# Talking-heads attention with a feed-forward block: other places for the loads of q, k, v and of the second weights, and for one batch's transposes

## The chip, the cores and the metric

The kernel runs on one core of a Trainium2 chip. Its time is the device time of one execution in microseconds. The kernel before took 603.37 us in the median of 13 runs, from 599.58 to 607.42.

## What is computed

For 8 batches of 12 heads with 448 positions of 64 elements, scores of all heads are mixed by a 12x12 matrix, go through a softmax, are mixed again by a second 12x12 matrix and multiply v. The result, 3584 rows of 768, goes through a feed-forward block with a squared ReLU and 2048 hidden columns.

```python
scores = scale * np.matmul(q, k.transpose(0, 1, 3, 2))
scores = np.einsum('bhij,hg->bgij', scores, w_pre)
scores = scores - np.max(scores, axis=-1, keepdims=True)
attn = np.exp(scores)
attn = attn / (np.sum(attn, axis=-1, keepdims=True) + 1e-09)
attn = np.einsum('bhij,hg->bgij', attn, w_post)
attn_out = np.matmul(attn, v)
...
h = np.maximum(x @ w_in, 0.0)
out = h * h @ w_out
```

All inputs and the output are float32 in memory; the loads convert to bf16 on the way into on-chip memory.

## The kernel before

**Tiles and pairs.** A tile is 10 query rows of one batch with all 12 heads, so 45 tiles make a batch and 360 make the whole. The main loop (L500) handles two tiles per pass, a *pair* `ds`; there are 180 pairs, 22.5 per batch, and a few closing passes. Loads are listed by tile number `i`, and tile `i` belongs to pair `i // 2`.

**One tile's way.** `load_qk` brings a third of the heads of k or q of a batch into the one staging tile `qkst` (L72 is where the DMA is issued, from GpSimd's queue, POOL). `turn_unit` transposes a third of the heads on TensorE (L182) and copies the result to `qT` and `kT` (L186, one copy on ScalarE and one on VectorE). `score_pair` (L319) computes scores of two heads for 128 rows (L329) and copies them to the tile `S` (L333). `gather` (L346, L357) is a DMA issued from SyncE's queue (SP) that reorders scores so that the 12 heads of a query lie on neighbouring partitions, in a tile `G`; there are 8 such tiles, and for the first 28 tiles of the run 6 more, which lie in the memory of the last quarter of the second weights (`w2_3`; the profile calls those gathers w<-S). `mix` (L361) multiplies a gathered pair by the first mixing matrix (L367), exponentiates on ScalarE (L372), takes the reciprocal of the sum on VectorE (L374) and scales on GpSimd (`d`, L376). `unmix` (L387), two pairs later (`LAG`), multiplies by the second matrix (L399) and copies to `at` (L404). When a third of a batch is unmixed, `av_unit` multiplies by v (L199), which gives columns of `xt`.

**The feed-forward block as filler.** Once a batch's attention is finished, its first feed-forward phase (`ffn1_unit`: products L251, ReLU on ScalarE L258, square on GpSimd L260) and then its second one (`ffn2_unit`: products L281, copy on VectorE L288, output DMA on SP's queue L271) are cut into units, and each pair runs some of them after its own work. So during most of the run each batch's pairs carry the feed-forward block of the batch before: from about pair 22.5 b + 5 to + 16 of batch b the first phase, from there to pair + 27 (the fifth pair of the next batch) the second one. In batch 0 the first phase of the batch itself runs in three parts as its columns become ready, up to pair 30; its second phase is from pair 30 to 49.

**What sets the order.** TensorE and GpSimd take their instructions in the order in which the program lists them (`manual_schedule`), so everything a pair lists on these engines, a load's issue included, stands in front of what follows. SP's queue holds gathers and output stores in order. `scores_for` issues at most one or two score pairs a pass, none in a pass that has a turn, and none whose heads have not been turned; `gathers_for` issues gathers up to 8 tiles ahead (14 in the head) and stops where scores are missing.

**Where the loads stand.** `at_load(i, ...)` puts a load at the start of the pass of tile i. Before the change:

| load | tile numbers | pairs |
|---|---|---|
| q, k of batch 1 (six thirds) | 9, 11, ... 19 | 4 to 9 |
| second weights (eight pieces of 256 rows) | 21, 23, ... 35 | 10 to 17 |
| v of batch 1 (four quarters) | 36 to 39 | 18, 18, 19, 19 |
| q, k of batch 2 | 40, 42, ... 50 | 20 to 25 |
| q, k of batch b + 2, b from 1 | 45 b + 22, ... + 32 | 22.5 b + 11 to + 16 |
| v of batch b + 1, b from 1 | 45 b + 34, ... + 40 | 22.5 b + 17 to + 20 |

`TURN` gives, counted from the pair in which a batch's tile 0 stands, the three pairs that turn the next batch's q and k: for the pair of batch 1 (pair 22) it is 7, 8, 9, so batch 2 is turned at pairs 29, 30 and 31.

Of the kernel before, what the change touches and what calls it, by code (L numbers as in the profile page):

```python
# [15 lines left out]
B, H, S, D = 8, 12, 448, 64  # L16
# [8 lines left out]
NT = 45  # L25
# [10 lines left out]
OFF = 64 - H * (IQ // 2)  # L36
SCALE = 1.0 / 8.0
FIRST_TURN = (15, 16, 17)
TURN = {0: FIRST_TURN, 1: (7, 8, 9), B: (1, 5, 8)}
EARLY = [10, 18, 25]  # L40
ROWS = [128, 128, 128, 64]

# [2 lines left out]
def kernel(  # L45
# [387 lines left out]
    with tc.manual_schedule(engines={PE, POOL}):  # L433
# [9 lines left out]
        def at_load(i, f, *args):  # L443
            loads.setdefault(i, []).append(lambda: f(*args))
# [2 lines left out]
            at_load(-1, load_w1, x)  # L447
        for x in range(4):
            at_load(-1 if x < 2 else 2, load_v, 0, x)
            at_load(36 + x, load_v, 1, x)  # L450
        for x in range(2, 8):
            at_load(1 + x, load_w1, x)
        for x in range(6):
            at_load(9 + 2 * x, load_qk, 1, x)
            at_load(40 + 2 * x, load_qk, 2, x)
        for x in range(8):
            at_load(21 + 2 * x, load_w2, x)
        for b in range(1, B):
            if b + 2 < B:
                for x in range(6):  # L460
                    at_load(NT * b + 22 + 2 * x, load_qk, b + 2, x)
            if b + 1 < B:
                for x in range(4):
                    at_load(NT * b + 34 + 2 * x, load_v, b + 1, x)
        nd = len(steps) // 2
        issued, gathered = [NPAIR + 3], [0]
        spans = [span_of(s) for s in steps]
# [32 lines left out]
        for ds in range(nd + LAG):  # L500
# [5 lines left out]
            for b, t in now2:  # L506
                if t == 0:
                    if b == 0:
                        at_step(ds + 6, (100, cg_unit))
                    if b + 1 < B:  # L510
                        for x in range(3):
                            turns[ds + TURN.get(b, TURN[B])[x]] = (b + 1, x)
            rest = ((NT + 1) // 2 + LAG + 2 - ds) % (NT / 2) + 1
# [70 lines left out]
```

## Time and profile before

| | |
|---|---|
| median of 13 runs | 603.37 us |
| profiled execution | 603.41 us |
| its span, first to last instruction | 601.6 us |
| mean granted TensorE clock | 0.978 |
| PE, DVE, ACT, POOL busy | 549.5, 409.2, 409.0, 400.2 us |
| software queue (loads, from POOL) | 23.60 MB, 29.4% of 16 engines |
| hardware queue of SP (gathers, output) | 49.35 MB, 35.6% of 16 engines |

PE is TensorE, DVE is VectorE, ACT is ScalarE, POOL is GpSimd, SP is SyncE; PEld is TensorE's loading of weights, which lies beside its matmuls. Engines work side by side, so the busy times don't add up to the span. A row of waits reads: engine, tile and line that waited, then what it waited for, total us, number of waits, longest. A row of groups reads: line, engine, operation, tiles, shapes, count, then busy us and mean ns of one, then the idle time before them and what ended it. These are rows for the instructions around the loads:

```profile
L376 POOL TENSOR_SCALAR d<-e_sb,rc 128x448 bf16<-128x448 f32 x360 | 226.5, 642 | 160.1 <-DVE rc L374 158.1
L260 POOL TENSOR_TENSOR h<-hr 128x448 bf16<-128x448 f32 (+2 forms) x136 | 114.0, 847 | 17.1 <-ACT hr L258 17.1
L72 POOL DMA_DIRECT2D qkst<-in_k_dram x24 | 16.0, 667 | 0.8 <-POOLq L568 0.8
L242 POOL DMA_DIRECT2D w<-in_moe_w_out_dram x8 | 6.0, 751 | 0.0
```

The last two are the time that GpSimd itself spends on issuing a load, not the time of the transfer.

### The profile page before, as it was taken

What the parts mean: (1) busy time and instruction counts of PE and PEld (TensorE: products, weight loads), DVE (VectorE), ACT (ScalarE), POOL (GpSimd) and SP (SyncE); (2) the same over time, 40 slices, a digit from 0 to 9 for tenths busy, and PEclk for the clock granted to TensorE, in tenths of its full rate; (3) what the DMA queues carried; (4) which work ended last, traced back from release to release, by engine and by line L of the source; (5) the groups of instructions that cost most, each with busy time, mean ns of one, the idle gap of its engine ahead of it and who ended that gap; (6) DMA issues with size and microseconds to landing.
All of it is one profiled execution on the core that took longest, in us unless ns stands there. A gap on an engine that the chain in (4) does not pass through costs nothing.

```text
span 601.6 us, 28171 instructions
## 1 busy us (share of the span) xinstructions
PE 549.5 (91%) x11810; PEld 312.2 (52%) x11810; DVE 409.2 (68%) x1050; ACT 409.0 (68%) x1223; POOL 400.2 (67%) x599
## 2 busy tenths in 40 slices
PE   3767788887999999999999999999999999999996
PEld 1534556643555455545555455545655555555554
DVE  6675577877886777766877687677877788754101
ACT  3656577876788767887688667876788768862420
POOL 5475577657568964898469954897478856882540
PEclk9888698999999999999999999999999999999999
DMA  9899999549755885489646885489543765442102
GB/s 141 134 222 186 190 171 170 98 64 188 161 123 112 152 159 122 98 136 144 142 109 106 148 165 112 88 151 159 128 102 73 122 145 122 80 76 66 30 17 76
DMA packets 83364, 74.98 MB, mean 125 GB/s; under 512 B 6436, under 2 KB 80164, under 8 KB 83236
## 3 DMA queue, kind: packets, MB, share of 16 engines
q1 hardware_dynamic: 51582, 49.35, 35.6%
q0 software_dynamic: 31264, 23.60, 29.4%
q8 instruction: 92, 1.51, 1.0%
q10 hardware_dynamic: 390, 0.22, 0.1%
q14 instruction: 36, 0.29, 0.1%
HBM read 47.20 MB, written 11.01 MB: 97 GB/s over the span
## 4 chain that ended last, share of the span: by engine, by line
PE 64%; DMA 13%; POOL 10%; DVE 4%; ACT 3%; SPq 1%; issue 1%; ACTq 0%; DVEq 0%
PE o_ps L281 23%; PE h_ps L251 18%; DMA G<-S 9%; PE at_ps L399 8%; PE ot_ps L199 6%; PE m_ps L367 5%; POOL d L376 4%; POOL h L260 4%; DMA w<-S 3%; PE s_ps L329 3%; DVE at L404 3%; PE tr_ps L182 2%; POOL qkst L72 2%; ACT e_sb L372 1%; SPq L357 1%
## 5 line engine op out<-in xcount | busy, mean ns | idle before, releaser
L376 POOL TENSOR_SCALAR d<-e_sb,rc 128x448 bf16<-128x448 f32 x360 | 226.5, 642 | 160.1 <-DVE rc L374 158.1
L404 DVE CAST at<-at_ps 128x480 bf16<-128x480 f32 x360 | 219.8, 650 | 59.2 <-PE at_ps L399 49.9
L372 ACT ACTIVATE e_sb<-m_ps 128x448 f32<-128x448 f32 x360 | 195.8, 558 | 37.1 <-PE m_ps L367 25.6
L251 PE MATMUL h_ps<-xt,w 128*128 128x448 bf16 (+2 forms) x960 | 164.5, 319 | 1.5 <-DVE at L404 0.9
L281 PE MATMUL o_ps<-w,h 128*128 128x384 bf16 (+1 forms) x1024 | 161.6, 327 | 0.1
L260 POOL TENSOR_TENSOR h<-hr 128x448 bf16<-128x448 f32 (+2 forms) x136 | 114.0, 847 | 17.1 <-ACT hr L258 17.1
L251 PEld LDWEIGHTS <-w 128*128 128x128 bf16 x960 | 80.4, 99 | 78.0 <-issue 28.6
L281 PEld LDWEIGHTS <-h 128*128 128x128 bf16 (+1 forms) x1024 | 82.5, 101 | 70.9 <-issue 25.6
L333 ACT CAST S<-s_ps 128x448 bf16<-128x448 f32 (+1 forms) x174 | 90.9, 542 | 34.7 <-PE s_ps L329 29.6
L333 DVE CAST S<-s_ps 128x448 bf16<-128x448 f32 (+1 forms) x174 | 104.3, 613 | 0.9 <-PE s_ps L329 0.9
L374 DVE RECIPROCAL rc<-sm 128x1 f32<-128x1 f32 x360 | 53.0, 157 | 64.2 <-ACT e_sb L372 61.6
L367 PE MATMUL m_ps<-G,pre 64*64 64x448 bf16 (+2 forms) x696 | 79.1, 357 | 18.9 <-DMA G<-S 12.6
L399 PEld LDWEIGHTS <-d 60*64 60x64 bf16 x5760 | 65.1, 110 | 58.4 <-issue 29.7
L399 PE MATMUL at_ps<-post,d 60*64 60x60 bf16 x5760 | 86.6, 195 | 8.8 <-POOL d L376 4.9
L258 ACT ACTIVATE hr<-h_ps 128x448 f32<-128x448 f32 (+2 forms) x160 | 74.0, 485 | 23.0 <-PE h_ps L251 11.9
L372 ACT ACTIVATION_READ_ACCUMULATOR e_sb<-m_ps 128x1 f32 x360 | 78.2, 217 | 0.0
L210 ACT ACTIVATE xt<-ot_ps,bvec 128x160 bf16<-128x160 f32 (+3 forms) x144 | 44.7, 384 | 47.7 <-PE ot_ps L199 37.1
L329 PE MATMUL s_ps<-kT,qT 64*64 64x448 bf16 x672 | 64.2, 372 | 0.7 <-ACT qT L186 0.2
L288 DVE COPY osb<-o_ps 128x384 f32<-128x384 f32 x48 | 26.0, 547 | 39.2 <-PE o_ps L281 39.0
L367 PEld LDWEIGHTS <-pre 64*64 64x64 bf16 x720 | 29.0, 107 | 43.1 <-issue 34.1
L199 PE MATMUL ot_ps<-at,v 128*64 128x160 bf16 (+4 forms) x1152 | 47.0, 233 | 1.4 <-DVE at L404 1.4
L199 PEld LDWEIGHTS <-v 128*64 128x64 bf16 x1152 | 39.5, 112 | 14.6 <-issue 14.0
(42 smaller groups left out, 215.8 us busy)
## 6 DMA issues: line engine op xcount, KB each, us to landing
G<-S SPq DMA_DIRECT2D x319, 105.0 KB
out_dram<-osb SPq DMA_DIRECT2D x48, 192.0 KB
v<-in_v_dram POOLq DMA_DIRECT2D x32, 192.0 KB, 5.2
qkst<-in_k_dram POOLq DMA_DIRECT2D x24, 224.0 KB, 5.8
qkst<-in_q_dram POOLq DMA_DIRECT2D x24, 224.0 KB, 6.0
w<-in_moe_w_in_dram POOLq DMA_DIRECT2D x8, 384.0 KB, 10.6
w<-in_moe_w_out_dram POOLq DMA_DIRECT2D x8, 384.0 KB, 9.4
out_dram<-osb SPq DMA_DIRECT2D x16, 96.0 KB
```

The source lines that it names most:

```text
L199: nc.tensor.matmul(ps[64 * hh:64 * hh + 64, TW * y + c0:TW * y + 2 + n], lhsT=vs[b][:, g, r, :], rhs=at[:, r, g, c0:2 + n], start=(y == 0 ...
L251: nc.tensor.matmul(ps[:, 0:n], lhsT=w1[ft // 4][:, c2, ft % 4 * 128:ft % 4 * 128 + 128], rhs=xts[b][:, c2, c0:c1], start=(c2 == 0), stop=( ...
L258: nc.scalar.activation(out=hr[:, 0:n], in_=ps[:, 0:n], func=ACT.Relu)
L260: square.tensor_tensor(out=h2ts[(b, ft)][:, c0:c1], in0=hr[:, 0:n], in1=hr[:, 0:n], op=ALU.mult)
L281: nc.tensor.matmul(dst, lhsT=h2ts[(b, ft)][:, mt * 128:mt * 128 + ROWS[mt]], rhs=w2[ft // 4][:, ft % 4, n2 * 384:(n2 + 1) * 384], start=(f ...
L329: nc.tensor.matmul(pss[hh][PR * z:PR * z + PR, 0:S], lhsT=qTs[b][rs, p, PR * j:PR * j + PR], rhs=kTs[b][rs, p, :], start=True, stop=True)
L333: copy(out=Sb[n][z0:z1, 2 * p + hh, :], in_=pss[hh][z0:z1, 0:S])
L367: nc.tensor.matmul(pss[y][64 * x:64 * x + 64, 0:S], lhsT=pre[rows, :], rhs=gs[x][rows, :], start=True, stop=True)
L372: nc.scalar.activation(out=e[:, :], in_=pss[y][:, 0:S], func=ACT.Exp, scale=SCALE, accum_out=sm[:, 0:1])
L376: nc.gpsimd.tensor_scalar(out=d[:, 0:S], in0=e[:, :], scalar1=rc[:, 0:1], scalar2=-1.0 / S, op0=ALU.mult, op1=ALU.add)
L399: nc.tensor.matmul(us[x][PR * z:PR * z + PR, c:c + HR], lhsT=d[rows, j:j + PR], rhs=post[rows, :], start=True, stop=True)
L404: nc.vector.tensor_copy(out=dst, in_=src)
```

## The change

```diff
-TURN = {0: FIRST_TURN, 1: (7, 8, 9), B: (1, 5, 8)}
+TURN = {0: FIRST_TURN, 1: (11, 13, 15), B: (1, 5, 8)}
...
         for x in range(4):
             at_load(-1 if x < 2 else 2, load_v, 0, x)
-            at_load(36 + x, load_v, 1, x)
+            at_load(46 + 2 * x, load_v, 1, x)
         for x in range(2, 8):
             at_load(1 + x, load_w1, x)
         for x in range(6):
-            at_load(9 + 2 * x, load_qk, 1, x)
-            at_load(40 + 2 * x, load_qk, 2, x)
+            at_load(11 + 2 * x, load_qk, 1, x)
+            at_load(56 + 2 * x, load_qk, 2, x)
         for x in range(8):
-            at_load(21 + 2 * x, load_w2, x)
+            at_load(24 + 4 * x, load_w2, x)
         for b in range(1, B):
             if b + 2 < B:
                 for x in range(6):
-                    at_load(NT * b + 22 + 2 * x, load_qk, b + 2, x)
+                    at_load(NT * b + 34 + 2 * x, load_qk, b + 2, x)
             if b + 1 < B:
                 for x in range(4):
-                    at_load(NT * b + 34 + 2 * x, load_v, b + 1, x)
+                    at_load(NT * b + 46 + 2 * x, load_v, b + 1, x)
```

No load and no computation is added or dropped. In pairs: q and k of batch 1 go from pairs 4 to 9 to pairs 5 to 10; the second weights from pairs 10 to 17 to every other pair from 12 to 26; v of batch 1 from pairs 18 and 19 to 23 to 26; q and k of batch 2 from pairs 20 to 25 to 28 to 33, and its turns from pairs 29, 30, 31 to 33, 35, 37; q and k of batches 3 to 7 go six pairs later, from the first to the second feed-forward phase; and v of batches 2 to 7 go six pairs later, into the first pairs of the next batch.

Because a turn holds back score pairs, the number of score pairs in passes 29 to 38 changes from 0, 0, 0, 2, 2, 1, 1, 1, 1, 1 to 1, 1, 1, 0, 0, 2, 0, 2, 0, 2, and the number of gathers in passes 32 and 33 from 0 and 4 to 2 and 2.

## The prediction

> Times in the windows below are us from the start of the profiled span. A "pair" is one pass of the loop over tile pairs; the profile shows two exponentials (L372) per pair, so counting them dates every pair: pair 0 starts at 21.7, pair 10 at 53.5, 18 at 82.6, 24 at 100.0, 33 at 128.6, 45 at 160.1 and the last, 179, at 545.8. A batch is 22.5 pairs.
>
> **What bounds the kernel now.** First I read the page's strips and its chain.
>
> ```profile
> PE   3767788887999999999999999999999999999996
> PEclk9888698999999999999999999999999999999999
> DMA  9899999549755885489646885489543765442102
> PE 64%; DMA 13%; POOL 10%; DVE 4%; ACT 3%; SPq 1%; issue 1%; ACTq 0%; DVEq 0%
> ```
>
> Each digit is 15 us. From slice 10 on TensorE is full. In the first ten it isn't, its clock is lower, and the DMA engines are full; the 13% that the chain gives to DMA are 78 us. In order of time, the chain passes through DMA transfers G<-S or w<-S nearly without a break from 25.9 to 81, again at 93 to 99.5 and at 131 to 150, and nowhere later. Next the waits of TensorE from 53.5 to 82.6 (pairs 10 to 17), and engine sums by stretch (stretch and length, then PE, PEld, DVE, ACT, POOL busy, granted clock, DMA share, GB/s):
>
> ```profile
> PE m_ps L367 <- DMA w<-S: 3.7, 4, 1.1
> PE m_ps L367 <- DMA G<-S: 2.3, 4, 1.0
> ...
> 53.50:82.60 29.10, 21.84 (x594) 15.12 (x583) 17.32 (x45) 17.53 (x59) 19.52 (x32) 0.82 1.01 191
> 82.60:105.00 22.40, 18.78 (x437) 13.32 (x435) 18.00 (x46) 17.12 (x61) 17.66 (x30) 0.92 0.96 165
> 105.00:125.00 20.00, 17.54 (x557) 12.49 (x555) 17.83 (x48) 17.16 (x60) 12.37 (x23) 1.00 0.46 87
> 125.00:160.00 35.00, 30.08 (x693) 15.88 (x691) 26.85 (x72) 23.51 (x76) 21.30 (x35) 1.00 0.83 155
> 160.00:225.00 65.00, 63.37 (x1490) 34.68 (x1488) 49.78 (x127) 51.00 (x151) 50.60 (x74) 1.00 0.70 134
> 225.00:290.00 65.00, 63.32 (x1355) 34.13 (x1352) 47.35 (x121) 49.68 (x147) 47.81 (x71) 1.00 0.69 129
> 290.00:357.00 67.00, 65.09 (x1418) 35.62 (x1416) 49.29 (x125) 50.51 (x151) 48.55 (x71) 1.00 0.69 130
> 357.00:423.00 66.00, 63.63 (x1446) 34.54 (x1444) 48.61 (x124) 49.41 (x146) 48.85 (x72) 1.00 0.69 128
> 423.00:488.00 65.00, 64.53 (x1419) 35.39 (x1417) 49.38 (x126) 50.40 (x151) 44.98 (x66) 1.00 0.57 112
> ```
>
> The first two rows read: mix (L367) waited 6.0 us in eight waits for its gathered tile while the DMA engines were at 1.01. TensorE takes its instructions in order, so whatever follows that matmul waits too. The last five rows are batches 2 to 6: TensorE idles 1.63, 1.68, 1.91, 2.37 and, in batch 6, only 0.47 us. Batch 6 is the one that loads no q and k any more (it still loads v): a trial of part of the change that the kernel itself contains.
>
> **Prices of transfers.** The software queue moved 23.60 MB in 29.4% of 601.6 us: 7.5 us of all 16 engines per MB, so 2.95 us for a load of second weights (384 KB), 1.72 for a third of q or k (224 KB), 1.48 for a quarter of v (192 KB). The hardware queue: 49.35 MB in 35.6%, 4.34 us per MB, so 0.47 us for a gather (105 KB) and 6.0 for a batch's output (1.38 MB).
>
> **Part A, second weights, pairs 10 to 17.** Before, one load per pair: 8 x 2.95 = 23.6, with 16 gathers 7.5, together 31.1 us of DMA work in 29.1 us. After, loads at pairs 12, 14 and 16 (8.9) and the last third of k/q of batch 1 at pair 10 (1.7): 18.1. DMA stops being full; what is late next are the engines of the row (TensorE 21.84 at a clock of 0.82, POOL 19.52 less five issues of 0.75). The gain lies between 0 and the idle 7.26; the nearest row is the 6.0 of waits. Some backlog from the first weights remains (loads of q and k issued from 33.7 to 44.3 took 15.4 to 18.5 us to land), so I take a bit over half: **-3.5**.
>
> **Part B, pairs 18 to 23.** Before, four quarters of v, four thirds and 12 gathers: 5.9 + 6.9 + 5.6 = 18.4 in 17.4 us. After, three second weights, one v: 8.9 + 1.5 + 5.6 = 16.0, and no backlog handed over. TensorE waited here for G 2.0 us in two waits; half of it: **-1.0** (0 to -2).
>
> **Part C, pairs 24 to 32.** The postponed work arrives: before 2 thirds and 18 gathers, 3.4 + 8.4 = 11.9 in 28.6 us; after two second weights, three v, five thirds: 5.9 + 4.4 + 8.6 + 8.4 = 27.3, or 0.95. That is the load of pairs 18 to 23 before, whose waits were 2.0 in 22 us: **+1.5** (0 to +3).
>
> **Part D, pairs 33 to 44.** Before 6 thirds, 4 v, 24 gathers and some of batch 0's output: 10.3 + 5.9 + 11.2 + 3.8 = 31.2 in 31.5 us, with G waits of 3.9 us in five. After 7 thirds, no v: 27.0, and nothing is loaded in pairs 34 to 38, where three of the waits lay. The order of the two programs shows a second thing. Before, turning batch 2 at pairs 29, 30, 31 withholds score pairs for three passes; pair 32 then issues no gather and pair 33 four, two of them a pair late, and the chain goes through two G at 131.4 to 143. With turns at 33, 35, 37 the score pairs come 1,1,1,0,0,2,0,2,0,2 and every pair issues its two gathers. The same 56 transposes (0.84 us of PE a turn) and copies (0.61 on DVE, 0.91 on ACT) are only moved. **-2.0** (0 to -4). Turn 0 has its k and q from pairs 28 and 29, over 10 us ahead, against 4 to 7 us to landing outside the head.
>
> **Part E, first feed-forward phases of batches 2 to 5's passes.** POOL issues there six q/k loads of 0.66 us between squares (L260, 0.94 a full one) and d (L376, 0.64). Rows: POOL is busy 13.11 of 14 us from 191 to 205 and 4.96 of 5 from 205 to 210, while TensorE idles 0.62 of those 5; from 160 to 423 TensorE waited for POOL d 4.0 us in 11. Taking the issues out is worth at most what batch 6 shows: mean idle 1.90 less 0.47, 1.43 a batch, 5.7 in four. Half, since the issues return where POOL must also still finish its squares: **-2.8**.
>
> **Part F, second phases.** POOL is busy some 60% of these (20.31 of 33.40 us from 272 to 305.4), and between d's it idles for rc (158 us in all): the six issues hide. v moves a further six pairs, still within the phase. The cost is in DMA: six thirds, 11 gathers and about half a batch's output in 5.5 pairs (16 us): 1.38 + 1.18 + 0.66 MB, 201 GB/s.
>
> ```profile
> 210.00:217.00 7.00, 6.69 (x149) 4.03 (x146) 4.97 (x13) 4.80 (x16) 6.57 (x11) 1.00 0.98 145
> 217.00:222.00 5.00, 5.00 (x104) 2.61 (x102) 4.05 (x12) 3.51 (x12) 1.73 (x3) 1.00 0.97 210
> ```
>
> Here v, output and gathers run together now: share 0.97, 210 GB/s, and TensorE doesn't wait for a gather. The Trainium skill ("DMA: Bandwidth & Descriptors", Specifications) gives 435 GB/s as ceiling of the fabric; by it 201 is under half, and F costs nothing. By the rows the engines are full at 190 to 210; the highest slice of the page is 222. The measurement decides: the stretch is at its edge. Gathers are issued 3.5 pairs (10 us) before use, which covers a 5 to 6 us landing; I take +0.3 for each of five batches: **+1.5** (0 to +22, rival 1).
>
> The same page's "Rules for kernel authors" speaks against the whole change: issue a DMA early, wait late. By it, later loads gain nothing and risk exposure. Rows: a load lands in 4 to 7 us outside the head, and the tightest use is four pairs (11 us) off: w2's last load at pair 26, its first product not before pair 30, its own quarter about pair 33. Issued early, the loads take the gathers' bandwidth. So I follow the rows, at no cost for lateness.
>
> Sum: -3.5 - 1.0 + 1.5 - 2.0 - 2.8 + 1.5 = **-6.3**. The profiled run took 603.41 (span 601.6), the median is 603.37, so the sum needs no shift: **597**. A higher clock in the head through less idling isn't counted.
>
> **Rivals.**
> 1. Starved gathers in the second phases, slower. In the head full engines meant eight waits of 0.75 us in eight pairs. If the 5.5 pairs of each of five batches waited 0.8 a pair: 22 us in place of 1.5, so 597 + 20.5 = 617; it cancels the gain from about 1.6 us a batch on. For: 201 GB/s against 190 to 210 at full. Against: the 210 GB/s row has no wait, and 10 us lead. Chance 0.16 (over 604).
> 2. The DMA waits of the head only hide another chain (scores, evacuations, a fixed order on TensorE), so A to D give 0, and E and F remain: 602. For: DVE 18.00 and ACT 17.12 of 22.40 in the second row. Against: the chain names DMA. Chance 0.22 (600 to 604).
> 3. DMA was the only limit of the head: A 6, B 2, C 0, D 4, E 5.7, F 0: 603.4 - 17.7 = 586. Chance 0.12 (under 592).
>
> The forecast (592 to 600) keeps 0.50. **Range** 589 to 606: half of rival 3 and all of rival 1 beyond 606 left out. A change under 0.5% can't be told from none here: faster (under 600.4) 0.50 + 0.12 + 0.04 of rival 2 = 0.66; same 0.18, the rest of rival 2; slower (over 606.4) 0.16.
>
> **What would show it.** A: pairs 10 to 17 in 25 to 26 us, DMA share there well under 1, w<-S waits gone. D: no 11 us of G in the chain near pair 33. E: idle of TensorE in batches 2 to 5 about 1.2. F: DMA near 1 in the second phases without G waits. Wrong if mix waits for G after 160, if pairs 24 to 32 lose more than 3, or if pairs 10 to 17 keep their 29 us with DMA no longer full.

## The result and the profile after

The changed kernel took 593.05 us in the median of 11 runs (588.23 to 595.83), the kernel before, measured beside it and pooled with its earlier runs, 603.05 in 48: a ratio of 0.9834, 95% interval 0.981 to 0.9858. The profiled execution is a long one, 596.94 us (span 595.2), 3.9 over the median; a possible reason stands at the end, under instruction fetch.

The strips and the chain of the page after:

```profile
PE   2876778889799999999999999999999999999996
PEclk9889979989999999999999999999999999999999
DMA  9899839976974499547963698449953477432002
PE 76%; DMA 12%; DVE 3%; ACT 3%; issue 2%; POOL 1%; ACTq 0%; SPq 0%
```

TensorE's share of the chain rises from 64 to 76%, GpSimd's (POOL) falls from 10 to 1%, and that of the transfers hardly moves (13 to 12%). The same view for batches 2 to 5 alone, first before, then after:

```profile
by line: PE o_ps L281 23.9%; PE h_ps L251 16.9%; POOL d L376 9.8%; PE at_ps L399 9.4%; POOL h L260 8.5%; PE ot_ps L199 7.4%; PE m_ps L367 5.5%; POOL qkst L72 3.8%; PE s_ps L329 3.4%; DVE at L404 3.1%; PE tr_ps L182 2.7%; issue 1.4%; ACT xt 
```

```profile
by line: PE o_ps L281 29.2%; PE h_ps L251 28.4%; PE at_ps L399 12.1%; PE ot_ps L199 8.1%; PE m_ps L367 7.4%; PE s_ps L329 5.0%; DMA G<-S 2.6%; PE tr_ps L182 2.5%; ACT xt L210 1.5%; DVE at L404 1.2%; issue 0.9%; ACT e_sb L372 0.8%; ACT hr L2
```

Before, GpSimd's d, its squares and its issue of loads carry 22% of these 263 us, the issue alone (qkst L72) 3.8%, which is 10 us. After, none of them stands in the line (the view cuts both lines off on the right; GpSimd has no entry in what is cut off after). The batches again, as rows of windows that begin and end with batches 2 to 6 (in the order of columns of the prediction; a packet counts for the DMA share in the stretch in which it starts, so a share can come out over 1):

```profile
157.30:223.40 66.10, 63.02 (x1404) 33.80 (x1406) 48.36 (x124) 50.55 (x150) 48.49 (x72) 0.97 0.67 131
223.40:287.60 64.20, 63.39 (x1443) 34.78 (x1444) 47.96 (x122) 49.18 (x147) 48.46 (x72) 1.00 0.70 132
287.60:353.20 65.60, 64.99 (x1427) 35.60 (x1429) 49.34 (x126) 50.26 (x151) 48.73 (x72) 1.00 0.69 133
353.20:416.60 63.40, 62.77 (x1442) 34.21 (x1443) 47.99 (x122) 49.27 (x146) 48.26 (x72) 1.00 0.71 134
416.60:481.40 64.80, 64.33 (x1419) 35.28 (x1417) 49.08 (x126) 50.26 (x151) 45.01 (x66) 1.00 0.60 118
```

The rows of the prediction begin and end at other places. Counted alike, from the exponential of a batch's first tile to that of the next, batches 3, 4 and 5 took 67.1, 66.2 and 67.0 us before and take 65.4, 64.4 and 64.7 after; batch 6 is as it was, 64.0 and 63.9. TensorE idles 0.8, 0.6 and 0.6 us in the rows of batches 3 to 5, and 3.1 us in that of batch 2, most of it in its first pairs. The pairs of the head, 10 to 17, 18 to 23, 24 to 32 and 33 to 44:

```profile
52.80:80.50 27.70, 18.07 (x595) 12.86 (x584) 17.54 (x45) 17.44 (x59) 16.41 (x27) 0.94 0.80 157
80.50:97.00 16.50, 14.61 (x336) 10.12 (x335) 14.87 (x39) 13.74 (x48) 11.45 (x20) 0.89 0.46 78
97.00:124.40 27.40, 23.18 (x619) 15.92 (x617) 22.46 (x59) 20.62 (x75) 23.81 (x42) 1.00 1.00 184
124.40:157.30 32.90, 29.78 (x736) 16.04 (x735) 26.27 (x69) 23.72 (x74) 18.72 (x31) 0.95 0.73 139
```

The DMA engines are no longer full in the first row, and full in the third. Dated by their exponentials, as in the prediction, the pairs took in the profiles of all kernels of the study that bear on the head (us, one execution each):

| kernel | 10-17 | 18-23 | 24-32 | 33-44 | 45-49 |
|---|---|---|---|---|---|
| before | 29.1 | 17.4 | 28.6 | 31.6 | 12.5 |
| after | 27.6 | 16.5 | 27.5 | 32.8 | 16.9 |
| after_again | 26.3 | 16.0 | 26.2 | 30.9 | 17.0 |
| head_only | 25.5 | 16.1 | 27.3 | 30.0 | 13.8 |
| w2_only | 25.4 | 20.0 | 28.5 | 32.1 | 12.5 |
| no_w2 | 29.4 | 15.2 | 24.9 | 30.7 | 16.0 |
| turn_late | 31.2 | 15.7 | 24.5 | 31.0 | 14.9 |
| steady_only (head as before) | 30.5 | 16.1 | 27.3 | 31.3 | 12.6 |

before and steady_only have the same head. Three kernels of the experiments below (pool_less, pool_busy, transfer_held) have the head of the changed kernel; with them its columns run, in six profiles of one head, from 24.2 to 27.6, 16.0 to 18.3, 24.9 to 27.8, 30.0 to 33.3 and 13.8 to 17.0. So a single entry is good to some 3 us; medians of runs decide where they can.

### The profile page after: what moved, and what is told of

The parts are those of the page before. It is cut to its first block, busy times and chain, and to the rows that moved or that the text cites. A ratio compares the mean times of both kernels' runs of the same rounds, so it can differ in the third digit from the quotient of the medians.

```text
span 595.2 us, 28172 instructions
## 1 busy us (share of the span) xinstructions
PE 544.2 (91%) x11810; PEld 308.7 (52%) x11810; DVE 408.9 (69%) x1050; ACT 407.8 (69%) x1223; POOL 399.8 (67%) x599
## 3 DMA queue, kind: packets, MB, share of 16 engines
q8 instruction: 92, 1.51, 1.0%
## 4 chain that ended last, share of the span: by engine, by line
PE 76%; DMA 12%; DVE 3%; ACT 3%; issue 2%; POOL 1%; ACTq 0%; SPq 0%
PE o_ps L281 25%; PE h_ps L251 24%; PE at_ps L399 9%; DMA G<-S 8%; PE ot_ps L199 6%; PE m_ps L367 6%; PE s_ps L329 4%; DMA w<-S 3%; DVE at L404 2%; PE tr_ps L182 2%; ACT xt L210 1%; ACT e_sb L372 1%; POOL d L376 0%; DVE h L260 0%; DVE osb L293 0%
## 5 line engine op out<-in xcount | busy, mean ns | idle before, releaser
L281 PE MATMUL o_ps<-w,h 128*128 128x384 bf16 (+1 forms) x1024 | 163.6, 330 | 0.1
L367 PE MATMUL m_ps<-G,pre 64*64 64x448 bf16 (+2 forms) x696 | 78.5, 361 | 17.5 <-DMA G<-S 11.3
L399 PEld LDWEIGHTS <-d 60*64 60x64 bf16 x5760 | 63.6, 110 | 56.0 <-issue 35.2
L399 PE MATMUL at_ps<-post,d 60*64 60x60 bf16 x5760 | 83.9, 195 | 7.8 <-issue 4.4
L258 ACT ACTIVATE hr<-h_ps 128x448 f32<-128x448 f32 (+2 forms) x160 | 74.0, 483 | 17.4 <-PE h_ps L251 10.6
L199 PE MATMUL ot_ps<-at,v 128*64 128x160 bf16 (+4 forms) x1152 | 45.8, 229 | 1.4 <-DVE at L404 1.4
L199 PEld LDWEIGHTS <-v 128*64 128x64 bf16 x1152 | 38.4, 109 | 14.5 <-issue 13.8
```

The source lines that it names most:

```text
L199: nc.tensor.matmul(ps[64 * hh:64 * hh + 64, TW * y + c0:TW * y + 2 + n], lhsT=vs[b][:, g, r, :], rhs=at[:, r, g, c0:2 + n], start=(y == 0 ...
L258: nc.scalar.activation(out=hr[:, 0:n], in_=ps[:, 0:n], func=ACT.Relu)
L281: nc.tensor.matmul(dst, lhsT=h2ts[(b, ft)][:, mt * 128:mt * 128 + ROWS[mt]], rhs=w2[ft // 4][:, ft % 4, n2 * 384:(n2 + 1) * 384], start=(f ...
L367: nc.tensor.matmul(pss[y][64 * x:64 * x + 64, 0:S], lhsT=pre[rows, :], rhs=gs[x][rows, :], start=True, stop=True)
L399: nc.tensor.matmul(us[x][PR * z:PR * z + PR, c:c + HR], lhsT=d[rows, j:j + PR], rhs=post[rows, :], start=True, stop=True)
```

## Experiments

### Which half of the change pays

**steady_only** and **head_only** part the change at the loop over later batches. steady_only starts from the kernel before:

```diff
-at_load(NT * b + 22 + 2 * x, load_qk, b + 2, x)
+at_load(NT * b + (22 if b == 1 else 34) + 2 * x, load_qk, b + 2, x)
-at_load(NT * b + 34 + 2 * x, load_v, b + 1, x)
+at_load(NT * b + (34 if b == 1 else 46) + 2 * x, load_v, b + 1, x)
```

head_only starts from the kernel after and has 34 and 46 for b == 1 alone, 22 and 34 for the others:

```diff
-at_load(NT * b + 34 + 2 * x, load_qk, b + 2, x)
+at_load(NT * b + (34 if b == 1 else 22) + 2 * x, load_qk, b + 2, x)
-at_load(NT * b + 46 + 2 * x, load_v, b + 1, x)
+at_load(NT * b + (46 if b == 1 else 34) + 2 * x, load_v, b + 1, x)
```

> Only the loads of q, k and v of batches 4 to 7 and 3 to 7 (the loop from its second batch on) move six pairs later; the head stays as before. If the profile of the changed kernel is typical (batches 2 to 5 shorter by 1.5 to 2.3 us each, together 7.3), this gives 603.0 - 7 = 596 and a ratio near 0.988. By the split of the prediction (E and F, -1.3) it gives 602, ratio 0.998.

> Everything up to pair 49 as in the changed kernel, the loads of later batches where they were before. If the later batches bring 7 of the 10 us, this gives about 600 (ratio 0.995). By the split of the prediction (A to D, -5.0) it gives 598, ratio 0.992.

steady_only took 595.6 against 602.58, ratio 0.9895 (0.985 to 0.994): -7.0. head_only took 599.08, 0.9949 (0.9929 to 0.997): -3.5. Together -10.5, and the whole change gave -10.0: the halves add up, and by the medians two thirds lie in the later batches (intervals -9.0 to -3.6 and -4.3 to -1.8), which the prediction had down for a fifth.

### What it is in the later batches: GpSimd's time or the transfer

Here are six pairs of batch 3 (79 to 84), before, then after. Five of its six loads of q and k used to be issued in them, and the first one just ahead, at 255.8:

```profile
258.90:275.20 16.30, 15.45 (x289) 7.24 (x288) 11.11 (x30) 12.83 (x39) 15.80 (x24) 1.00 0.84 150
```

```profile
258.40:272.80 14.40, 14.40 (x288) 6.90 (x287) 10.74 (x29) 12.54 (x38) 13.39 (x20) 1.00 0.47 85
```

GpSimd was busy 15.80 of 16.30 us, and with the loads 2.4 us of its work went. Its timeline before shows issue, d and squares without a gap:

```profile
268.52 0.66 POOL L72 DMA_DIRECT2D qkst<-in_k_dram  x1
269.22 1.25 POOL L376 TENSOR_SCALAR d<-e_sb,rc 128x448 bf16<-128x448 f32 x2
270.45 1.82 POOL L260 TENSOR_TENSOR h<-hr 128x448 bf16<-128x448 f32 x2
272.22 0.66 POOL L72 DMA_DIRECT2D qkst<-in_q_dram  x1
272.92 1.25 POOL L376 TENSOR_SCALAR d<-e_sb,rc 128x448 bf16<-128x448 f32 x2
```

But the DMA share fell too, 0.84 to 0.47, so two causes fit. **pool_busy** and **pool_less** put GpSimd time back without transfers, **transfer_only** and **transfer_held** transfers without GpSimd time, all from the kernel after. pool_busy (pool_less has 4 in place of 6):

```diff
+scrap = consts.tile([P, 4], F32, name="scrap")
+def busy():
+    for _ in range(6):
+        nc.gpsimd.memset(scrap[:, :], 0.0)
...
 at_load(NT * b + 34 + 2 * x, load_qk, b + 2, x)
+if b > 1:
+    at_load(NT * b + 22 + 2 * x, busy)
```

> The changed kernel; in the first phases of batches 2 to 6, where the q and k loads used to be issued, GpSimd clears a tiny scratch tile six times per former load, which takes about as long as issuing it (0.66 us) and moves no data by DMA. If GpSimd's time on the issue was the cost, batches 2 to 5 lose most of what they gained, 5 to 7 us: 598 to 600. If it was the transfer's share of the DMA engines, nothing changes: 593. Batch 6 gets the clears too though it had no q or k loads, which adds at most 2 us under the first theory.

> As pool_busy, with four clears in place of six. In pool_busy 24 groups of six took 14.6 us and 6.9 between them, 0.90 us a group, and batches 2 to 5 were 11.2 us longer than in the changed kernel's profile. If GpSimd's time is what counts, four clears take 0.60 us a group and cost two thirds of that, 7.5 us, about what the loads' issue cost before (0.66 us each): 600 to 602. If the number of instructions in the way (their order and semaphores) counts more than their time, it stays near 606.

pool_busy took 606.69, ratio 1.007 (1.0036 to 1.0104), pool_less 600.94, 0.998 (0.9953 to 1.0006). In one point the first expectation describes its kernel wrongly: the clears go to batches 2 to 5 only. pool_busy overshot its number in part because a group of clears was longer than an issue (0.90 us against 0.66). Batch 3's six pairs in pool_busy, with the DMA share as low as after and GpSimd full again (15.43 us busy and some 1.7 between its clears), are even longer than before:

```profile
260.00:277.00 17.00, 15.63 (x290) 7.31 (x288) 11.23 (x30) 12.94 (x39) 15.43 (x49) 1.00 0.45 79
```

In place of the clears, transfer_only and then transfer_held have copies to a scratch array in memory:

```diff
+nc.sync.dma_start(out=scrap[P * n:P * n + P, :], in_=w1[0][:, 0:3, :].rearrange("p c f -> p (c f)"))
```

```diff
+for y in range(2):
+    n, p = divmod(issued[0] - 1 - y, NPAIR)
+    z = 2 * x + y
+    nc.sync.dma_start(out=scrap[P * z:P * z + P, :].rearrange("p (h s) -> p h s", h=2), in_=Sb[n][:, 2 * p:2 * p + 2, :])
```

> The changed kernel, with a plain transfer added wherever a q or k load of batches 4 to 7 used to be issued: 384 KB of first weights copied to a scratch array in memory from SyncE's queue, 1.7 us of all 16 DMA engines by the hardware queue's price, as much as the former load (1.72), and no GpSimd time. If GpSimd's time was the cost in the first phases, batches 2 to 5 keep their length: 593, within 1.5. If the load on the DMA engines (or the gathers behind it) was the cost, they lose 1.5 to 2 us each again: 599 to 601.

> The changed kernel with transfers in the first phases again, this time of data that come into being there: at each place where a q or k load of batches 4 to 7 used to be issued, SyncE copies the two newest pairs of score rows (2 x 224 KB) to a scratch array in memory, 2.0 us of all 16 DMA engines by the hardware queue's price, against 1.72 of the former load, and no GpSimd time. If GpSimd's time was the cost, batches 2 to 5 stay within 0.5 us of the changed kernel's: 593, within 1.5. If the transfers were, they lose 1.5 to 2 us each: 599 to 601.

transfer_only took 616.13 (1.0208, 1.0167 to 1.0248) and says nothing on its question: SyncE's order isn't written by hand, the weights were there to be copied, and all 24 copies were issued between 14.7 and 87.3 us. Pairs 5 to 17 took 65.3 us there against 45.5 after; from pair 50 on every stretch is as after. So 9.4 MB more in the head cost 20 us; whether by full engines or because the copies stand in SyncE's queue in front of gathers isn't parted.

transfer_held did place its copies (185.9 to 208.1, 252.2 to 274.8 and so on) and took 610.28, 1.0117 (1.0079 to 1.0155). By its text that speaks for transfers; the pairs say where. Summed over batches 2 to 5 (pairs 56 to 61, 79 to 84, 101 to 106 and 124 to 129, then the five after each), from the profiles:

| kernel | six pairs of the former loads | the next five pairs |
|---|---|---|
| before | 66.40 | 59.80 |
| after, and after_again | 60.03, 60.03 | 58.81, 58.83 |
| steady_only | 60.03 | 58.86 |
| pool_less (0.58 us a group) | 64.18 | 59.40 |
| pool_busy (0.90 us a group) | 68.57 | 60.08 |
| transfer_held | 61.71 | 71.51 |

With 0.9 to 1.4 times the issues' GpSimd time and no transfer, the six pairs lose 4.15 and 8.54 us; the loads themselves cost 6.37. Per us of GpSimd that is 0.30 (of 24 x 0.58), 0.40 (of 24 x 0.90) and 0.40 (of 24 x 0.66). More bytes than the loads moved, without GpSimd, cost 1.68 there, and nothing at all in batches 2 and 4. In batches 3 and 5 the first load is issued one pair earlier; counted from there (78 and 123), the sums are 67.79 before, 61.57 after, 65.90 in pool_less, 69.67 in pool_busy and 61.53 in transfer_held, so the copies cost nothing in any batch. So **GpSimd's time on the issue is the main cause** in these pairs. A line through the two kernels with clears gives 5.2 of the 6.37 at the issues' 15.84 us; the other 1.1 us is not shown to be GpSimd's. (Of what the medians of the two kernels with clears lie over the changed one, 2 to 4 us are outside these stretches and not explained.) The 12.7 us that transfer_held loses come after them, in the second phase: its copies stand in SyncE's queue in front of gathers, and where the moved q and k loads begin, the gathers are late; whether the queue or the engines held them up isn't parted. TensorE's waits for gathers from 275 to 430 and batch 3's five pairs:

```profile
PE m_ps L375 <- DMA G<-S: 6.2, 4, 3.6
```

```profile
275.30:294.10 18.80, 16.41 (x299) 8.86 (x298) 10.15 (x27) 9.77 (x32) 9.28 (x16) 0.91 0.84 165
```

That is what the prediction's rival 1 feared, starved gathers in a second phase. In the changed kernel the same five pairs take 14.7 us in each batch:

```profile
272.80:287.50 14.70, 14.39 (x298) 8.13 (x296) 11.07 (x29) 9.68 (x32) 10.57 (x18) 1.00 0.90 158
```

### What it is in the head

**w2_only** changes from the kernel before, **no_w2** undoes from the kernel after, the one line of the second weights. **turn_late** takes from the change only the turns of batch 2, the loads of q and k that the staging tile then forces later, and v of batch 2. The edits of w2_only and turn_late:

```diff
-at_load(21 + 2 * x, load_w2, x)
+at_load(24 + 4 * x, load_w2, x)
```

```diff
-TURN = {0: FIRST_TURN, 1: (7, 8, 9), B: (1, 5, 8)}
+TURN = {0: FIRST_TURN, 1: (11, 13, 15), B: (1, 5, 8)}
-at_load(NT * b + 22 + 2 * x, load_qk, b + 2, x)
+at_load(NT * b + (34 if b == 1 else 22) + 2 * x, load_qk, b + 2, x)
-at_load(NT * b + 34 + 2 * x, load_v, b + 1, x)
+at_load(NT * b + (46 if b == 1 else 34) + 2 * x, load_v, b + 1, x)
```

> The kernel before with the second weights alone spread over fourteen pairs. If the DMA engines bound pairs 10 to 17, as the prediction's part A says, those pairs take 25 to 26 us in place of 29.1, and the time falls by 2 to 3.5 us (600 to 601). If pairs 10 to 17 were held by something else as well (in the changed kernel's profile TensorE stops there in mid-sequence for 2.2 and 3.3 us with nothing to wait for), they keep 27.5 us or more and the time stays within 1.5 us of 603.

> The changed kernel with the second weights back in pairs 10 to 17. If their spread frees pairs 10 to 17 (25.5 us with it in two of the profiles, 29 to 30.5 without), and is worth what it gives only together with the later v and q, k loads, pairs 10 to 17 return to 29 or more and the time rises by 2 to 3.5 us: 595 to 596.5. If only the later loads of v, q and k matter in the head, it stays at 593.

> The kernel before with batch 2 turned at pairs 33, 35, 37, and, since the staging tile is taken until then, q and k of batch 3 and v of batch 2 six pairs later; all else as before. By part D the pairs 33 to 44 lose their waits for gathers and get 1.5 to 2 us shorter: 601 to 601.5. If those waits went with the load of the DMA engines in earlier pairs, it stays at 603.

w2_only: 602.6, ratio 1.0011 (0.9987 to 1.0035), no gain. Pairs 10 to 17, then 18 to 23, and the waits of the second stretch:

```profile
54.20:79.70 25.50, 18.59 (x599) 13.96 (x588) 17.16 (x44) 17.50 (x59) 17.76 (x29) 0.93 0.78 153
79.70:99.70 20.00, 14.88 (x338) 10.20 (x336) 16.85 (x41) 13.63 (x48) 15.69 (x27) 0.91 1.09 178
```

```profile
PE m_ps L367 <- DMA G<-S: 3.7, 1, 3.7
```

Part A came in its size, 3.6 us off pairs 10 to 17 with the DMA share down from 1.01 to 0.78. Over all profiles the two heads don't overlap there: 29.1 to 31.2 us in the four with the early weights, 24.2 to 27.6 in the seven with the late ones (transfer_only and the two with other turns of batch 1 left aside). Its picture came only in part: the waits for G went, but those for w<-S, 3.7 us before, did not. In the changed kernel:

```profile
PE m_ps L367 <- DMA w<-S: 3.4, 4, 1.2
```

In w2_only they are 3.2 us in three. And TensorE's busy time there fell from 21.84 to 18.59 us for some 600 matmuls in both, at a granted clock of 0.93 against 0.82, a term that the prediction did not count; how much of the 3.6 is the clock's isn't parted. Then the postponed weights meet the loads of v and of batch 2, the share is 1.09, one gather comes 3.7 us late, and 2.6 of the gain are gone at once.

no_w2: 593.3, 0.9839 (0.9796 to 0.9881), the same as the whole change. Its pairs 10 to 17 return to 29.4 us, but 18 to 32 take 40.1, where six profiles of the changed head have 42.2 to 45.3. The line of the second weights moves some 3 us from one place to another, and no gain from it shows in the time (w2_only -0.8 to +2.1 us).

turn_late: 599.43, 0.9954 (0.9913 to 0.9996), about -3 of the head's -3.5, with the weights, v and batch 2's loads all where they were. Pairs 24 to 32 and 33 to 44, before, then in turn_late:

```profile
100.00:128.60 28.60, 25.63 (x733) 18.66 (x733) 21.73 (x58) 22.52 (x78) 17.03 (x31) 0.94 0.51 96
128.60:160.10 31.50, 27.09 (x620) 13.93 (x617) 24.61 (x65) 21.83 (x70) 19.54 (x32) 1.00 0.91 172
```

```profile
99.30:123.80 24.50, 22.99 (x619) 16.04 (x619) 21.26 (x59) 20.30 (x76) 18.45 (x33) 1.00 0.65 131
123.80:154.80 31.00, 28.89 (x735) 15.62 (x734) 25.90 (x68) 23.92 (x74) 18.34 (x30) 1.00 0.67 129
```

Three turns with their 168 transposes leave the first stretch and score pairs come in (114 matmuls fewer, and 115 more in the second). They leave a stretch that gets 4.1 us shorter and enter one that doesn't get longer, since its waits for gathers are gone, 3.9 us before and 0.2 here. Loads moved along with the turns (v of batch 2 left that stretch, q and k of batch 3 went to its second half, and its DMA share fell from 0.91 to 0.67), so whether the turns or the loads ended these waits isn't parted. turn_late pays back 2.4 of the 4.1 in pairs 45 to 49 (14.9 against 12.5), where q, k of batch 3 and v of batch 2 now arrive together with output. In the changed kernel it is 4.4 (1.3 to 4.5 in the six profiles of its head); these are its waits of mix there:

```profile
156.81 0.38 PE L367 MATMUL m_ps<-G,pre 64*64 64x448 bf16 x3 [0.67 <-DMA G<-S]
160.26 0.37 PE L367 MATMUL m_ps<-G,pre 64*64 64x448 bf16 x1 [1.24 <-DVE qT L186]
161.81 0.38 PE L367 MATMUL m_ps<-G,pre 64*64 64x448 bf16 x3 [1.18 <-DMA G<-S]
```

### Stops with nothing to wait for

In the changed kernel's pairs 16 and 17 TensorE stops in the middle of a run of equal instructions. Its timeline:

```profile
71.72 0.61 PE L182 MATMUL tr_ps<-ident,qkst 64*64 64x64 bf16 x52 [2.18 <-issue]
72.15 0.37 PE L367 MATMUL m_ps<-G,pre 64*64 64x448 bf16 x4
72.45 1.00 PE L251 MATMUL h_ps<-xt,w 128*128 128x160 bf16 x12
73.39 1.85 PE L199 MATMUL ot_ps<-at,v 128*64 128x160 bf16 x48
75.17 0.28 PE L399 MATMUL at_ps<-post,d 60*64 60x60 bf16 x12
78.73 0.48 PE L399 MATMUL at_ps<-post,d 60*64 60x60 bf16 x20 [3.28 <-issue]
```

Between the two stops lie 52 + 4 + 12 + 48 + 12 = 128 matmuls, with their weight loads 256 instructions. In all profiles but that of transfer_only one or more of the same few places stops for over 0.45 us. **turn_spread** takes the turns of batch 1 apart, and was run again beside the changed kernel.

```diff
-FIRST_TURN = (15, 16, 17)
+FIRST_TURN = (13, 15, 17)
```

> The changed kernel with batch 1 turned at pairs 13, 15, 17 in place of 15, 16, 17. TensorE stops in pairs 16 and 17 exactly 256 instructions apart, each time 2.4 us after a 16 KB packet of the instruction queue starts. If TensorE outruns its instruction fetch where three turns follow each other, spreading them shortens the two stops (5.5 us in the changed kernel's profile, 1.0 to 3.6 in the others) and the time falls by 1 to 3 us: 590 to 592. If the stops come from the DMA engines being full, whatever TensorE does, they stay and the time stays at 593.

> The changed kernel on the same chip as turn_spread_again: 593, ratio 0.982 to 0.985.

> The changed kernel with batch 1 turned at pairs 13, 15, 17, beside the changed kernel on the same chip. If the two stops of TensorE in pairs 16 and 17 are worth 1 to 3 us in most executions, this is 1 to 3 us under the changed kernel; if they were long only in the one profile, under 1 us.

turn_spread took 591.43 (0.982, 0.9784 to 0.9855) and 592.06 (0.9819, 0.9781 to 0.9857), the changed kernel beside the second 594.54 (0.9846, 0.9802 to 0.989). The intervals overlap, so a gain over the changed kernel isn't shown. Nor are the stops gone: one profile has only short ones (four, 1.05 us at most), the other 3.07 us at pair 17 and 2.66 at pair 33. Spreading these turns isn't a cure; whether the stops need full DMA engines stays open. transfer_only, whose engines are full from 30 to 92 us, has none; its TensorE waits for gathers instead, 17.5 us in pairs 10 to 17.

## The prediction, step by step

The forecast of 597 in 589 to 606 holds the 593.05, and the likeliest case was the right one. Its terms were less good than their sum: -6.3 was forecast, -10.0 came. That this still lies in the range owes something to luck: the head was forecast 1.5 us too good (-5.0 against -3.5), the later batches 5.7 us not good enough.

- **E and F (-1.3) were mis-sized; they measured -7.0.** The mechanism of E was right, shown by pool_busy and pool_less. The size failed at the word "half": issues that return in the second phase were thought to take back half of what they had saved. No such cost shows (the five pairs after the former loads: 59.80 before, 58.81 after, though five issues of q and k came in for three or four of v), so the whole of E came. Its upper end, 5.7 from TensorE's idle time, was also short of the 6.4 us in the six pairs alone. The rows of pairs 79 to 84 show why idle time is no bound: of the 1.9 us that they lost, only 0.85 was idle, and the other 1.05 stood in TensorE's busy time, 15.45 us before against 14.40 for one matmul less. The page had shown more in the chain by line, which the prediction didn't use; its line before ends

```profile
PE o_ps L281 23%; PE h_ps L251 18%; DMA G<-S 9%; PE at_ps L399 8%; PE ot_ps L199 6%; PE m_ps L367 5%; POOL d L376 4%; POOL h L260 4%; DMA w<-S 3%; PE s_ps L329 3%; DVE at L404 3%; PE tr_ps L182 2%; POOL qkst L72 2%; ACT e_sb L372 1%; SPq L357 1%
```

  with 2% for the issue at L72. The line of batches 2 to 5 has it at 3.8% of 263 us: 10 us in which the end hung on GpSimd issuing a load. An idle row shows only where an engine stopped; a chain also shows whom it followed.
- **F** took +0.3 a batch for starved gathers, and none came in batches 3 to 5. The measurement that was to decide, "full at 190 to 210", held for its mix of transfers only: the share reached 0.90 at 158 GB/s without a wait, and the 201 that F reckoned with did not come. That the danger is real transfer_held shows. It did come in one place, pairs 45 to 49, 1 to 4.5 us over the 12.5 before, which the prediction had not priced.
- **A** (-3.5) was right in its place (3.6 in w2_only) and zero in the sum. Its way of adding was at fault: the DMA work that left A's pairs was charged too little in C (+1.5), and B (-1.0) reckoned with a gain where it cost time. With late turns and early weights (turn_late, no_w2) the pairs of C take 24.5 and 24.9 us and those of B 15.7 and 15.2; with late turns and late weights they take 26.8 and 16.8 in the mean of six profiles, 2.2 and 1.3 more.
- **B** (-1.0) can't be told from the scatter of the same head (17.4 in one profile, 16.1 in the other).
- **D** (-2.0) named two causes, fewer loads and turns that no longer withhold scores for three pairs in a row. turn_late moves both and measures -3 (interval -5.2 to -0.2) for them together. Its sign came: the 11 us of G in the chain near pair 33 are gone, in turn_late and in the changed kernel. The place was wrong: pairs 24 to 32 got shorter, and 33 to 44 took the turns for nothing.
- **The Trainium skill's rule** ("DMA: Bandwidth & Descriptors", Rules for kernel authors) on issuing a load early and waiting late didn't decide: no wait for a late load shows, and in the later batches it was the issue's place on a busy engine that counted, which that rule leaves out.

## What to carry to other kernels

A load has two prices, the DMA engines' time and the issuing engine's: look at which engine is full where the load is issued, and move the issue to a phase where that engine idles. A transfer moved out of a full stretch is not gone; add up the stretch that receives it, and measure the edit alone and undone before crediting it. To bound what freeing an engine brings, take its share of the chain in that stretch (10 us here, of which 6.4 came), not the idle time of the engine that waits for it.

## What was not expected of the hardware

- **Instruction fetch.** The instruction queue moved 92 packets, 1.51 MB, in every run, 16 KB each. If each holds 256 instructions, they make 23552, and TensorE's records of matmuls and weight loads number 23620. TensorE's stops of over 0.45 us without a releaser fall a multiple of 256 instructions apart, to within the few records that a trace lacks, in every profile that has more than one, and end 2.2 to 3.1 us after such a packet starts. That points to the fetch of instructions as what TensorE waited for; no run changed the fetch itself. They sum to 1.5 us before, 6.6 and 4.8 in two profiles of the changed kernel, and 0 to 7.8 in the others; the 6.6 may be why the changed kernel's profiled run lies 3.9 over its median. The Trainium skill ("Runtime: NRT & Kernel Launch", Instruction fetch mechanics) states blocks of 16 KiB or 256 instructions and calls the cost of crossing a block mostly hidden. The block size agrees; in this kernel's head, where short matmuls use up 256 instructions in under 4 us, a crossing showed up to 3.3 us.
- **"Full" DMA engines move very different amounts.** In transfer_only the slices of 15 us from 30 us on reach 227, 265, 253 and 258 GB/s, where the kernel before has 222 at most, and the changed kernel shows a share of 1.00 at 184 GB/s. The share says full; the rate at which it is full depends on what is moved.
